# The last piece's tail takes in an output product and a convolution as diagonal products, and the front's loads and conversions are put in another order

## The chip, the cores and the metric

The kernel runs on one core of a Trainium2 chip. The time is the device time of one launch in microseconds, the median of three runs. The engines are named as in the profile: TensorE (PE), VectorE (DVE), ScalarE (ACT), GpSimd (POOL) and SyncE (SP), which issues all the DMAs here.

## The reference

Three layers follow each other for 4 batches of 768 tokens with 384 channels: a gated linear attention with 8 heads of 48, a layer with a Fourier mix and an MLP of 1536 hidden channels, and a gated projection with a short causal convolution.

```python
for t in range(S):
    state = alpha[:, :, t, :, None] * state + np.einsum('bhd,bhe->bhde', k[:, :, t], v[:, :, t])
    y[:, :, t] = np.einsum('bhd,bhde->bhe', q[:, :, t], state)
...
mixed = np.real(np.fft.fft(np.fft.fft(x, axis=1), axis=2))
u = x + mixed
un = (u - mu) / np.sqrt(var + 1e-06)
ch = np.maximum(un @ w_ch1, 0.0) @ w_ch2
x = u + ch
...
for k in range(K):                       # K = 5
    gate_pre += conv_w[k][None, None, :] * xp[:, k:k + S, :]
gate = 1.0 / (1.0 + np.exp(-gate_pre))
out = gate * (x @ w_val) @ w_out
```

## The kernel before

Each batch goes through four stages: attention (six steps of 128 tokens), the Fourier mix, the MLP and the gate. MLP and gate work on pieces of 256 tokens, three to a batch, so there are twelve pieces. Channels lie on the partitions, in three blocks of 128 (`KD`). A product of full precision is made of three products with halves: high weight by high value, low weight by high value, high weight by low value (`mm3`, L648; high and low are `xh`, `xl`).

**The front** is the attention of batch 0 and the start of its Fourier mix, up to the first MLP product. `first` (L384) goes through eight strings of letters, `FIRST` (L44), one string a step, and emits for each letter one part: `A` VectorE's scans of a step, `B` its transposes and score products, `U` and `S` the state products (L335) and the state's update (L346, L351), `D` the output products (L366, L372), `0` to `2` transposes back (`turn`, L472), `f` to `h` the folds, `p` and `r` parts of the Fourier product (`dft_part`, L514). The letters `q`, `v` and `a` issue the loads of queries with keys and decays, of `vu` and of `va`. `l` issues up to four loads of weight chunks (L199), as far as buffers are free. `w` takes the next part of a weight conversion.

Weights come as 64-bit numbers in 24 chunks of 128x384 for w1 and w2, 7 more for the last weights. For a chunk VectorE makes a 32-bit number with three operations (L222, L225, L229), ScalarE rounds it to the high half (L233), and the low half is the rest: in the front two products of TensorE with the identity and with its negative (L242, L243) and a ScalarE copy (L244), later one subtraction on VectorE (L238). In the front `w` converts up to two staged chunks in three parts. From the first MLP piece on `convert_one` converts one chunk at every second step, together with the rest of the chunk before. The tap weights `cw` are a small chunk of 128x15 among the last seven.

**The order of the work.** The program is emitted in one order and each engine works through its instructions in that order; waits come from buffers and data. In the pieces, `run` (L846) emits an MLP step by step, and between the steps the next batch's attention, the norm of the next piece, the gate of the piece before and conversions.

**The end.** The gate of piece 10 ends with the output product, two times nine products of 384 columns (L759), a copy and a transfer; these lie between steps of the MLP of piece 11. Then `last_gate` (L766) does the gate of piece 11 alone. The MLP's last products finish channel block 2 first, then 0 and 1 (`LAST`). For block 2 the five taps of the convolution run on ScalarE and GpSimd (L792, L794), for the others on VectorE (L800, L802); the low halves `xl` come from GpSimd and VectorE; then the value products (L811), the sigmoids, the gating (L816), the halves of the gated values (L817, L819) and the output product (L825). PSUM tiles have the names `aux` (4 buffers), `mm` (2) and `ch`.

Of the kernel before, what the change touches and what calls it, by code (L numbers as in the profile page):

```python
# [43 lines left out]
FIRST = ("Alwwlqwwl", "BlaAlUwqwSvl", "lBDAwwllUaqvlSw", "BwlwwAwDallwUvSq", "AllylDBwUSavx", "BwAlDUSlawwv", "BawDlU0lSww1lfl", "lDg2wpllrh")  # L44
# [20 lines left out]
class Main:  # L65
# [630 lines left out]
    def gate(self, b, p):  # L696
# [45 lines left out]
        for j in range(KD):  # L742
# [6 lines left out]
            yield  # L749
        yield  # L750
# [14 lines left out]

    def last_gate(self, b, p):  # L766
# [8 lines left out]
        xh, xl = (self.pair(b * NPC + p + 2, [P, KD, NK]) for _ in range(2))  # L775
        gh, gl = (self.pair(b * NPC + p + 3, [P, KD, NK]) for _ in range(2))
# [3 lines left out]

        for j in LAST:
# [3 lines left out]
            if j == LAST[1]:  # L785
                nc.gpsimd.tensor_tensor(out=xl[:, j], in0=x2[:, j], in1=xh[:, j].bitcast(F32), op=ALU.subtract)
            if j != LAST[0]:
                continue
            for k in range(KC):
                xs, w = tap(j, k)  # L790
                m = self.t([P, NK], "tmp", 3) if k else gs[:, j]
                nc.scalar.activation(out=m, in_=xs, func=AF.Copy, scale=w)  # L792
                if k:
                    nc.gpsimd.tensor_tensor(out=gs[:, j], in0=gs[:, j], in1=m, op=ALU.add)  # L794
            nc.gpsimd.tensor_tensor(out=xl[:, j], in0=x2[:, j], in1=xh[:, j].bitcast(F32), op=ALU.subtract)
        for k in range(KC):
            for j in LAST[1:]:
                xs, w = tap(j, k)
                if k == 0:
                    nc.vector.tensor_scalar(out=gs[:, j], in0=xs, scalar1=w, scalar2=None, op0=ALU.mult)  # L800
                else:
                    nc.vector.scalar_tensor_tensor(out=gs[:, j], in0=xs, scalar=w, in1=gs[:, j],  # L802
                                                   op0=ALU.mult, op1=ALU.add)
        j = LAST[2]
# [8 lines left out]
        for j in LAST:  # L813
            nc.scalar.activation(out=gs[:, j], in_=gs[:, j], func=AF.Sigmoid)
# [316 lines left out]
```

## Time and profile before

| | |
|---|---|
| median of 3 runs | 639.39 us (634.35 to 640.05) |
| the profiled execution's own time | 641.17 us |
| its span, first to last instruction | 639.1 us |
| granted clock of TensorE, mean | 0.959 |
| busy: TensorE, VectorE, ScalarE, GpSimd | 585.1, 430.1, 244.5, 155.4 us |

The busy times are sums over stages with different limits. The profiled execution lies 1.8 us above the median; a time that is worked out from its rows is set against 641.17 first. A granted clock of 1.00 is 2.4 GHz, one of 0.50 is 1.2 GHz, and a value between them is a mix of both in that stretch.

### The profile page before, as it was taken

What the parts mean: (1) busy time and instruction counts of PE and PEld (TensorE: products, weight loads), DVE (VectorE), ACT (ScalarE), POOL (GpSimd) and SP (SyncE); (2) the same over time, 40 slices, a digit from 0 to 9 for tenths busy, and PEclk for the clock granted to TensorE, in tenths of its full rate; (3) what the DMA queues carried; (4) which work ended last, traced back from release to release, by engine and by line L of the source; (5) the groups of instructions that cost most, each with busy time, mean ns of one, the idle gap of its engine ahead of it and who ended that gap; (6) DMA issues with size and microseconds to landing.
All of it is one profiled execution on the core that took longest, in us unless ns stands there. A gap on an engine that the chain in (4) does not pass through costs nothing.

```text
span 639.1 us, 15952 instructions
## 1 busy us (share of the span) xinstructions
PE 585.1 (92%) x6626; PEld 547.0 (86%) x6626; DVE 430.1 (67%) x951; ACT 244.5 (38%) x582; POOL 155.4 (24%) x332
## 2 busy tenths in 40 slices
PE   3767899797999999999999999999999999999984
PEld 2546768686998899899999999899998999999973
DVE  6988778899836658975763939878556444453642
ACT  2333442224463264353543243434443343423221
POOL 0000215103126033123321324323231232322220
PEclk9868998789899999999999999999999999999996
DMA  9746351646143346533425346533321122000000
GB/s 339 279 137 229 108 173 11 200 144 164 51 138 71 124 125 115 171 99 89 135 75 92 103 125 142 157 110 94 115 63 48 49 71 88 15 9 26 9 27 30
DMA packets 29602, 69.50 MB, mean 109 GB/s; under 512 B 5200, under 2 KB 15952, under 8 KB 29520
## 3 DMA queue, kind: packets, MB, share of 16 engines
q1 hardware_dynamic: 29520, 68.38, 36.5%
q8 instruction: 54, 0.88, 0.6%
q14 instruction: 28, 0.23, 0.1%
HBM read 63.64 MB, written 4.73 MB: 107 GB/s over the span
## 4 chain that ended last, share of the span: by engine, by line
PE 68%; DVE 21%; DMA 4%; POOL 2%; issue 2%; ACT 2%; SPq 1%; DVEq 0%; POOLq 0%
PE ch L651 7%; PE mm L651 7%; PE ch L653 7%; PE ch L652 6%; PE mm L653 6%; PE mm L652 6%; PE aux L759 5%; PE aux L514 3%; PE aux L559 3%; DVE w L295 3%; DVE w L288 2%; PE aux L318 2%; PE aux L651 2%; PE aux L653 2%; PE aux L652 2%
## 5 line engine op out<-in xcount | busy, mean ns | idle before, releaser
L651 PE MATMUL ch<-hh,w2h 128*128 128x256 f32 x432 | 130.2, 301 | 0.2 <-ACT hh L672 0.2
L651 PE MATMUL mm<-hl,w1h 128*128 128x256 f32 x432 | 128.5, 298 | 1.0 <-ACT hl L608 1.0
L653 PE MATMUL ch<-hlo,w2h 128*128 128x256 f32 x432 | 122.9, 285 | 1.5 <-DVE hlo L674 1.5
L652 PE MATMUL ch<-hh,w2l 128*128 128x256 f32 x432 | 122.8, 284 | 0.0
L653 PE MATMUL mm<-hl,w1h 128*128 128x256 f32 x432 | 121.4, 281 | 0.0
L652 PE MATMUL mm<-hl,w1l 128*128 128x256 f32 x432 | 121.3, 281 | 0.0
L674 DVE SCALAR_TENSOR_TENSOR hlo<-mm,hh 128x512 fp32r<-128x512 f32 x72 | 49.5, 687 | 88.4 <-ACT hh L672 88.2
L651 PEld LDWEIGHTS mm<-hl,w1h 128*128 128x128 f32 x432 | 81.8, 189 | 4.0 <-ACT hl L608 1.4
L651 PEld LDWEIGHTS ch<-hh,w2h 128*128 128x128 f32 x432 | 82.5, 191 | 2.8 <-ACT hh L672 0.4
L653 PEld LDWEIGHTS ch<-hlo,w2h 128*128 128x128 f32 x432 | 82.7, 191 | 1.9 <-DVE hlo L674 1.9
L652 PEld LDWEIGHTS ch<-hh,w2l 128*128 128x128 f32 x432 | 82.7, 191 | 0.8
L652 PEld LDWEIGHTS mm<-hl,w1l 128*128 128x128 f32 x432 | 82.0, 190 | 0.8
L653 PEld LDWEIGHTS mm<-hl,w1h 128*128 128x128 f32 x432 | 81.9, 190 | 0.3 <-DVE hl L611 0.3
L672 ACT ACTIVATE hh<-mm 128x512 fp32r<-128x512 f32 x72 | 42.5, 591 | 58.7 <-PE mm L653 58.4
L726 DVE SCALAR_TENSOR_TENSOR ga<-u,cw,ga 128x256 f32<-128x256 f32 x132 | 58.0, 499 | 0.0
L748 POOL TENSOR_TENSOR hl<-ga,hl 128x256 fp32r<-128x256 f32 x33 | 25.5, 779 | 97.2 <-ACT hl L747 97.2
L617 POOL TENSOR_TENSOR tmp<-tmp,tmp 128x256 f32<-128x256 f32 x24 | 20.3, 846 | 101.3 <-ACT tmp L616 100.4
L380 POOL COPY x<-x 128x1 f32<-128x1 f32 x24 | 11.8, 493 | 123.8 <-ACT x L377 123.8
L318 PEld LDWEIGHTS aux<-w 48*64 48x64 f32 x768 | 27.5, 149 | 15.6 <-issue 8.2
L318 PE MATMUL aux<-w 48*64 48x64 f32 x768 | 30.9, 237 | 10.7 <-DVE w L298 6.0
L759 PE MATMUL aux<-wvo,hl 128*128 128x384 f32 x198 | 38.4, 337 | 0.0
L759 PEld LDWEIGHTS aux<-wvo,hl 128*128 128x128 f32 x198 | 33.8, 188 | 0.1
(178 smaller groups left out, 1166.1 us busy)
## 6 DMA issues: line engine op xcount, KB each, us to landing
qka<-in_qka_dram SPq DMA_DIRECT2D x23, 772.5 KB, 5.9
ck<-in_w_dram SPq DMA_DIRECT2D x24, 384.0 KB, 3.4
vu<-in_vu_dram SPq DMA_DIRECT2D x24, 192.0 KB, 3.6
u<-in_w_dram SPq DMA_DIRECT2D x12, 384.0 KB, 6.2
va<-in_va_dram SPq DMA_DIRECT2D x24, 192.0 KB, 4.0
ck<-in_al_dram SPq DMA_DIRECT2D x12, 384.0 KB, 3.3
out_dram<-ga SPq DMA_DIRECT2D x24, 192.0 KB, 1.9
w<-in_cs_dram SPq DMA_DIRECT2D x6, 579.0 KB, 5.3
```

The source lines that it names most:

```text
L295: nc.vector.tensor_tensor_scan(out=pre, data0=al[:, : A_W - 1], data1=self.starts, initial=0.0, op0=ALU.mult, op1=ALU.add)
L318: nc.tensor.matmul(out=sc[j * 64 : j * 64 + 64, cs], lhsT=kt[hs, cs], rhs=qt[hs, cs], start=True, stop=True)
L514: self.nc.tensor.matmul(out=pa[: d1 - d0, g * 193 : g * 193 + n], lhsT=self.eo[g][:, t, m, d0:d1], rhs=self.cs[g][:, t, m, :n], start=t == ...
L617: nc.gpsimd.tensor_tensor(out=ss, in0=ss, in1=sq, op=ALU.add)
L651: nc.tensor.matmul(out=out, lhsT=w[0][:, k, cols], rhs=xh, start=first, stop=False)
L652: nc.tensor.matmul(out=out, lhsT=w[1][:, k, cols], rhs=xh, start=False, stop=False)
L653: nc.tensor.matmul(out=out, lhsT=w[0][:, k, cols], rhs=xl, start=False, stop=last)
L672: nc.scalar.activation(out=hh, in_=hp, func=AF.Relu)
L674: nc.vector.scalar_tensor_tensor(out=hl, in0=hp, scalar=0.0, in1=hh.bitcast(F32), op0=ALU.max, op1=ALU.subtract)
L726: nc.vector.scalar_tensor_tensor(out=gs[:, j], in0=xs, scalar=w, in1=gs[:, j], op0=ALU.mult, op1=ALU.add)
L748: nc.gpsimd.tensor_tensor(out=gl[:, j], in0=gs[:, j], in1=gh[:, j].bitcast(F32), op=ALU.subtract)
L759: nc.tensor.matmul(out=po[:, :DM], lhsT=lh[:, k, ts], rhs=rh[:, k, :], start=n == 0, stop=n == 8)
```

## The change

At the end: the gate of piece 10 stops ahead of its output product and leaves its two operands to the last gate. `last_gate` runs this product itself, one half (`before(0)`) ahead of the value products and one (`before(1)`) behind them. The convolution of block 1 (`LAST[2]`) becomes five products of TensorE in FP32, each tap a diagonal matrix times a shifted slice; GpSimd builds the diagonals in `taps`. The taps of blocks 2 and 0 and all low halves are VectorE's, and the value products go block by block of their input. The last product takes the blocks in the order 1, 2, 0. In the front `FIRST` is another table.

```diff
-FIRST = ("Alwwlqwwl", "BlaAlUwqwSvl", "lBDAwwllUaqvlSw", "BwlwwAwDallwUvSq", "AllylDBwUSavx", "BwAlDUSlawwv", "BawDlU0lSww1lfl", "lDg2wpllrh")
+FIRST = ("Aqwwlwl", "aBwAqUwwSv", "BAwDwUaqvSw", "wBAwwwaDlwUvSq", "AlyllDBwUSavx", "BwAlDUSlawwwv", "aBwDlU0Sw1lf", "lgDwp2hr")
...
+        if self.tail and b * NPC + p + 2 == B * NPC:
+            self.rest = (b, p, gh, gl)
+            return
...
+    def taps(self):
+
+        self.diag = self.t([P, KC, P], "qka", 2)
+        for k in range(KC):
+            self.nc.gpsimd.tensor_scalar(out=self.diag[:, k], in0=self.ident, scalar1=self.cw[:, LAST[2], k : k + 1],
+                                         scalar2=None, op0=ALU.mult)
...
         for j in LAST:
-            nc.vector.tensor_tensor(out=gs[:, j], in0=ch[j], in1=rs, op=ALU.mult)
-            nc.vector.tensor_tensor(out=x2[:, j], in0=x2[:, j], in1=gs[:, j], op=ALU.add)
+            m = self.t([P, NK], "tmp", 3)
+            nc.vector.tensor_tensor(out=m, in0=ch[j], in1=rs, op=ALU.mult)
+            nc.vector.tensor_tensor(out=x2[:, j], in0=x2[:, j], in1=m, op=ALU.add)
             nc.scalar.activation(out=xh[:, j], in_=x2[:, j], func=AF.Copy)
...
+            if j == LAST[0]:
+                conv(j, 0)
+        before(0)
+        values(xh, LAST[0])
         for k in range(KC):
...
+            nc.tensor.matmul(out=cv[:, :NK], lhsT=self.diag[:, k], rhs=tap(LAST[2], k)[0],
+                             start=k == 0, stop=k == KC - 1)
+        for k in LAST[1:]:
+            values(xh, k)
         for j in LAST:
...
+            nc.vector.tensor_tensor(out=xl[:, j], in0=x2[:, j], in1=xh[:, j].bitcast(F32), op=ALU.subtract)
+            conv(LAST[0], 1 + LAST.index(j))
+        for k in LAST:
+            values(xl, k)
+        before(1)
+        conv(LAST[1], 0)
+        conv(LAST[0], 4)
+        for k in range(1, KC):
+            conv(LAST[1], k)
+        os = self.t([P, NK // P, DM], "w", 5)
+        nc.scalar.activation(out=os[:, 0], in_=po[0][:, :DM], func=AF.Copy)
+        nc.scalar.activation(out=gs[:, LAST[2]], in_=cv[:, :NK], func=AF.Sigmoid)
+        nc.scalar.activation(out=gs[:, LAST[0]], in_=gs[:, LAST[0]], func=AF.Sigmoid)
+        nc.scalar.activation(out=gs[:, LAST[1]], in_=gs[:, LAST[1]], func=AF.Sigmoid)
+        order = (LAST[2], LAST[0], LAST[1])
```

Here `before(t)` is the nine products of the old L759 for one half, `values(x, k)` the value products of input block `k` for all three output blocks, and `conv(j, k)` one tap on VectorE.

TensorE at the end of the program, before: the last channel products of the MLP (`ch`), then the value products (`aux`, `mm` from the halves `hl` and the weights `wvo`).

```order
L651 MATMUL ch_1063_7787<-hh_8031,w2h 128x256
L652 MATMUL ch_1063_7787<-hh_8031,w2l 128x256
L653 MATMUL ch_1063_7787<-hlo_8033,w2h 128x256
L811 MATMUL aux_8113<-hl_1087_8072,wvo_1089 128x256 x2
L811 MATMUL mm_8111<-hl_1087_8072,wvo_1089 128x256 x2
L811 MATMUL mm_8112<-hl_1087_8072,wvo_1089 128x256 x2
```

The same place now, from the end of the first half of the old output product (L801) on; `qka` holds the halves of the values and the diagonals.

```order
L801 MATMUL aux_8051<-wvo_1179,hl_1071_7869 128x384 x2
L801 MATMUL aux_8051<-wvo_1179,hl_1072_7870 128x384
L807 MATMUL aux_8055<-qka_8048,wvo_1179 128x256 x2
L807 MATMUL mm_8053<-qka_8048,wvo_1179 128x256 x2
L807 MATMUL mm_8054<-qka_8048,wvo_1179 128x256 x2
L828 MATMUL aux_8056<-u_6193,qka_8041 128x256 x5
L807 MATMUL aux_8055<-qka_8048,wvo_1179 128x256 x2
```

Nine products that stood in the MLP now follow the last channel product, and the five diagonal products stand behind the value products of the first input block.

VectorE in the front, before: step 3, from its scans (L288 to L298) to the state's update (L346); `hl_61_386` takes two chunks, and two more were converted just ahead of the scans.

```order
L288 SCALAR_TENSOR_TENSOR w_377<-qka_199,ends 128x520
L292 RECIPROCAL starts<-w_377 128x8
L293 TENSOR_TENSOR w_378<-qka_199,w_377 128x512
L295 SCALAR_TENSOR_TENSOR w_377<-qka_199,starts 128x520
L298 TENSOR_TENSOR w_378<-qka_199,w_377 128x512
L222 TENSOR_SCALAR hl_61_386<-u_103 128x384 x2
L225 SCALAR_TENSOR_TENSOR hl_61_386<-u_103,hl_61_386 128x384 x2
L229 SCALAR_TENSOR_TENSOR hl_61_386<-u_103,hl_61_386 128x384 x2
L346 TENSOR_TENSOR sp_459<-st_322,pend_278 128x192
```

The same step now; `hl_51_330` is the step's only chunk.

```order
L222 TENSOR_SCALAR hl_51_330<-hl_8_113 128x384
L225 SCALAR_TENSOR_TENSOR hl_51_330<-hl_8_113,hl_51_330 128x384
L319 TENSOR_TENSOR w_333<-aux_340,mask 128x512
L288 SCALAR_TENSOR_TENSOR w_358<-qka_177,ends 128x520
L292 RECIPROCAL starts<-w_358 128x8
L293 TENSOR_TENSOR w_359<-qka_177,w_358 128x512
L295 SCALAR_TENSOR_TENSOR w_358<-qka_177,starts 128x520
L298 TENSOR_TENSOR w_359<-qka_177,w_358 128x512
L229 SCALAR_TENSOR_TENSOR hl_51_330<-hl_8_113,hl_51_330 128x384
L346 TENSOR_TENSOR sp_443<-st_320,pend_245 128x192
```

In this step one chunk is converted in place of four. Up to the first MLP product it is 15 chunks in place of 18, and the three others are converted in the first two pieces.

VectorE in the first MLP piece, before: the second attention step's scans there, with the conversion of `cw` ahead of their last operation (L298).

```order
L295 SCALAR_TENSOR_TENSOR w_1297<-qka_1002,starts 128x520
L222 TENSOR_SCALAR u_103<-u_103 128x15
L225 SCALAR_TENSOR_TENSOR u_103<-u_103 128x15
L229 SCALAR_TENSOR_TENSOR cw<-u_103 128x15
L298 TENSOR_TENSOR w_1298<-qka_1002,w_1297 128x512
L674 SCALAR_TENSOR_TENSOR hlo_1330<-mm_1305,hh_1328 128x512
```

The same place now.

```order
L295 SCALAR_TENSOR_TENSOR w_1276<-qka_974,starts 128x520
L222 TENSOR_SCALAR hl_205_1294<-u_103 128x384
L225 SCALAR_TENSOR_TENSOR hl_205_1294<-u_103,hl_205_1294 128x384
L229 SCALAR_TENSOR_TENSOR hl_205_1294<-u_103,hl_205_1294 128x384
L238 TENSOR_TENSOR w2l<-hl_197_1236,w2h 128x384
L298 TENSOR_TENSOR w_1277<-qka_974,w_1276 128x512
```

A weight chunk stands where `cw` stood, and `cw` is converted behind the next attention step's scans.

## Rows read from the trace of the kernel before

**Rows 1.** Busy time by stretch; start:end, length, each engine, clock, DMA share, GB/s.

```profile
0.00:70.00 70.00, 44.86 (x813) 34.70 (x813) 58.14 (x132) 22.84 (x63) 5.49 (x17) 0.85 0.71 248
...
88.00:170.00 82.00, 68.72 (x924) 63.49 (x924) 75.75 (x151) 26.38 (x64) 19.17 (x39) 0.88 0.46 128
...
580.00:615.00 35.00, 35.00 (x290) 35.00 (x289) 14.49 (x33) 7.89 (x14) 7.53 (x19) 1.00 0.08 16
615.00:639.10 24.10, 12.21 (x60) 10.53 (x59) 11.89 (x24) 5.94 (x15) 4.73 (x6) 0.78 0.06 21
```

**Rows 2.** Timeline of VectorE, 36 to 49 us; start, length, instructions, [idle before, released by].

```profile
36.61 0.62 DVE L222 TENSOR_SCALAR hl<-u 128x384 int32<-128x384 int32 x2
...
39.02 0.35 DVE L346 TENSOR_TENSOR sp<-st,pend 128x192 f32<-128x192 f32 x1
...
48.58 0.36 DVE L351 TENSOR_TENSOR st<-mm,sp 128x192 f32<-128x192 f32 x1 [3.20 <-PE mm L335]
```

**Rows 3.** Timeline of TensorE, 24 to 89 us.

```profile
24.11 1.11 PE L335 MATMUL mm<-vu,w 64*64 64x48 f32 x32 [3.22 <-DMA vu<-in_vu_dram]
...
44.26 1.65 PE L242 MATMUL ch<-hl,ident 128*128 128x384 f32 x2
...
47.75 0.77 PE L335 MATMUL mm<-vu,w 64*64 64x48 f32 x32
...
69.99 0.44 PE L472 MATMUL aux<-ident,x 128*128 128x128 f32 x2 [1.69 <-POOL x L380]
...
88.99 0.38 PE L651 MATMUL mm<-hl,w1h 128*128 128x256 f32 x1 [0.96 <-ACT hl L608]
```

**Rows 4.** Timeline of VectorE, 97 to 119 us.

```profile
97.39 0.35 DVE L222 TENSOR_SCALAR hl<-w 128x384 int32<-128x384 int32 x1
...
99.31 0.15 DVE L625 TENSOR_SCALAR nv<-aux 128x2 f32<-128x2 f32 x1
...
118.41 0.17 DVE L222 TENSOR_SCALAR u<-u 128x15 int32<-128x15 int32 x1 [2.13 <-DMA u<-in_cw_dram]
```

**Rows 5.** Waits of TensorE, 88 to 165 us; who for whom, total, times, longest.

```profile
PE aux L318 <- DVE w L607: 4.6, 1, 4.6
PE aux L318 <- DVE w L298: 3.5, 1, 3.5
```

**Rows 6.** Timeline of the output product of piece 10, 604 to 608 us.

```profile
604.93 1.75 PE L759 MATMUL aux<-wvo,hl 128*128 128x384 f32 x9
...
606.35 0.19 PEld L651 LDWEIGHTS ch<-hh,w2h 128*128 128x128 f32 x1
606.52 0.28 PE L651 MATMUL ch<-hh,w2h 128*128 128x256 f32 x1
...
607.59 1.73 PE L759 MATMUL aux<-wvo,hl 128*128 128x384 f32 x9
```

**Rows 7.** Timeline of the tail, 616 to 633 us.

```profile
616.48 0.28 PE L653 MATMUL ch<-hlo,w2h 128*128 128x256 f32 x1
...
620.19 4.74 DVE L802 SCALAR_TENSOR_TENSOR ga<-u,cw,ga 128x256 f32<-128x256 f32 x8
...
626.00 0.42 DVE L816 TENSOR_TENSOR ga<-aux,ga 128x256 f32<-128x256 f32 x1 [0.74 <-PE aux L811]
...
626.93 5.56 PE L825 MATMUL aux<-wvo,hl 128*128 128x384 f32 x18 [0.61 <-ACT hl L817]
...
632.53 0.56 DVE L832 COPY ga<-aux 128x384 f32<-128x384 f32 x1 [4.44 <-PE aux L825]
```

**Rows 8.** Busy time by stretch in the tail, columns as in rows 1.

```profile
623.00:625.30 2.30, 0.33 (x3) 0.13 (x2) 2.26 (x6) 0.74 (x2) 0.00 (x0) 0.90 0.01 4
625.30:631.00 5.70, 5.08 (x16) 4.74 (x17) 2.09 (x6) 1.16 (x4) 0.00 (x0) 0.50 0.01 3
```

**Rows 9.** Chain of work that ended last, the first norm's FP32 products; start, length, what.

```profile
86.73 1.31 PE aux L593 x6
```

**Rows 10.** Timeline of VectorE, taps of piece 10's convolution.

```profile
596.16 2.46 DVE L726 SCALAR_TENSOR_TENSOR ga<-u,cw,ga 128x256 f32<-128x256 f32 x6
```

More of the change, by code (lines that the diff above doesn't have):

```diff
@@ L43 @@
 LAG_RS = 3
[L44 removed]
+FIRST = ("Aqwwlwl", "aBwAqUwwSv", "BAwDwUaqvSw", "wBAwwwaDlwUvSq", "AlyllDBwUSavx", "BwAlDUlSawwwv", "aBwDlU0Sw1lf", "lgDwp2hr")
 ORDER = "Bb.Aa..Dt.m.Cvc.q."
@@ L774, in last_gate @@
         gs = self.t([P, KD, NK], "ga", 1)
-        xh, xl = (self.pair(b * NPC + p + 2, [P, KD, NK]) for _ in range(2))
-        gh, gl = (self.pair(b * NPC + p + 3, [P, KD, NK]) for _ in range(2))
+        xhl = self.t([P, 2, KD, NK], "qka", 2, F32R)
+        xh, xl = xhl[:, 0], xhl[:, 1]
+        gh, gl = (self.pair(b * NPC + p + 1, [P, KD, NK]) for _ in range(2))
         def tap(j, k):
             return u[:, j, o + k : o + k + NK], self.cw[:, j, k : k + 1]
+        b1, p1, gh1, gl1 = self.rest
@@ new lines, in last_gate, with before, values @@
+        po = [self.aux() for _ in range(NK // P)]
+        va = [self.mm(), self.mm(), self.aux()]
+        cv = self.aux()
+        def before(t):
+            for k in range(KD):
+                for n, (lh, rh) in enumerate(((gh1, self.wo[0]), (gh1, self.wo[1]), (gl1, self.wo[0]))):
+                    nc.tensor.matmul(out=po[t][:, :DM], lhsT=lh[:, k, t * P : (t + 1) * P], rhs=rh[:, k, :],
+                                     start=k == 0 and n == 0, stop=k == KD - 1 and n == 2)
+        def values(x, k):
+            for j in LAST:
+                for w in self.wv if x is xh else self.wv[:1]:
+                    nc.tensor.matmul(out=va[j][:, :NK], lhsT=w[:, k, j * P : (j + 1) * P], rhs=x[:, k],
+                                     start=x is xh and k == LAST[0] and w is self.wv[0], stop=x is xl and k == LAST[2])
@@ L784, in last_gate @@
             nc.scalar.activation(out=xh[:, j], in_=x2[:, j], func=AF.Copy)
[L785 to L794, printed above, removed]
@@ L795, in last_gate @@
-            nc.gpsimd.tensor_tensor(out=xl[:, j], in0=x2[:, j], in1=xh[:, j].bitcast(F32), op=ALU.subtract)
-        for k in range(KC):
[L797 to L803, printed above, removed]
@@ L804, in last_gate @@
-        j = LAST[2]
-        nc.vector.tensor_tensor(out=xl[:, j], in0=x2[:, j], in1=xh[:, j].bitcast(F32), op=ALU.subtract)
-        va = [self.mm(), self.mm(), self.aux()]
-        for x, ws in ((xh, self.wv), (xl, self.wv[:1])):
-            for k in LAST:
-                for j in LAST:
-                    for w in ws:
-                        nc.tensor.matmul(out=va[j][:, :NK], lhsT=w[:, k, j * P : (j + 1) * P], rhs=x[:, k],
-                                         start=x is xh and k == LAST[0] and w is ws[0], stop=x is xl and k == LAST[2])
@@ L816, in last_gate @@
+        order = (LAST[2], LAST[0], LAST[1])
+        for j in order:
             nc.vector.tensor_tensor(out=gs[:, j], in0=va[j][:, :NK], in1=gs[:, j], op=ALU.mult)
             nc.scalar.activation(out=gh[:, j], in_=gs[:, j], func=AF.Copy)
-        for j in LAST:
+        nc.scalar.activation(out=os[:, 1], in_=po[1][:, :DM], func=AF.Copy)
+        for t in range(NK // P):
+            r = b1 * S + p1 * NK + t * P
+            nc.sync.dma_start(out=self.ap["out"][r : r + P, :], in_=os[:, t])
+        for j in order:
@@ L819, in last_gate @@
             nc.vector.tensor_tensor(out=gl[:, j], in0=gs[:, j], in1=gh[:, j].bitcast(F32), op=ALU.subtract)
         po = [self.aux() for _ in range(NK // P)]
-        for k in LAST:
+        for k in order:
             for t in range(NK // P):
@@ L825, in last_gate @@
                     nc.tensor.matmul(out=po[t][:, :DM], lhsT=lh[:, k, ts], rhs=rh[:, k, :],
-                                     start=k == LAST[0] and n == 0, stop=k == LAST[2] and n == 2)
+                                     start=k == order[0] and n == 0, stop=k == order[2] and n == 2)
         for t in range(NK // P):
@@ L854, in run @@
         self.check_jobs()
+        self.tail = True
         self.head, self.pa, self.n_rest = True, None, 0
@@ L920, in run @@
                 pass
+        self.taps()
         self.last_gate(*pieces[-1])
@@ L1017, in general @@
         nc = self.nc
+        self.tail = False
         with ExitStack() as c:
```

9 lines of the change are left out of this document (7 added, 2 removed).

## The prediction

> **What bounds the kernel now.** I read first the busy time by stretch [rows 1]. From 0 to 70 us (attention of the first batch, called the front here) VectorE works 58.1 of 70 us and TensorE only 44.9. From 88 to 170 us (the first two pieces of the MLP, with weight conversions and the attention of the next batch beside them) VectorE works 75.8 of 82 us and TensorE loses 13 us. From 580 to 615 us TensorE is without a gap at full clock. From 615 us to the end it works 12.2 of 24.1 us at a mean granted clock of 0.78. So there are three limits: VectorE in the front, VectorE again from 88 to 170 us, and a chain through all engines in the tail. The timelines and the waits then tell who waits for whom in each.
>
> **Tail.** The change removes 18 products of the piece before the last (L759) from the last MLP, two runs of nine. From the start of the first run to the next MLP product it is 1.59 us (604.93 to 606.52) [rows 6], for both 3.18. TensorE has no gap there [rows 1], so the last channel product, which ends at 616.76 us (616.48 + 0.28) [rows 7], ends at 613.58. The products that feed it are not nearer: each takes hidden values that were made a step earlier, as before.
>
> Before, TensorE then waited at each step for ScalarE, GpSimd and VectorE: it was busy 0.33 of 2.3 us from 623.0, and from 625.3 to 631 the granted clock was 0.50, the lower level of 1.2 GHz [rows 8]. The 18 output products L825 ran there, 5.56 us from 626.93 [rows 7].
>
> After, work that depends on nothing late stands in these holes. I add it up in TensorE's new order, at the prices of rows at full clock: nine products of 384 columns 1.59, nine of 256 columns 1.07 (606.52 to 607.59) [rows 6], six FP32 passes of 256 columns 1.31 [rows 9], which make three products, so 0.44 each.
> - first half of the old output product: 1.59
> - six value products of the first block: 0.71
> - five diagonal FP32 products: 2.18
> - twelve value products: 1.43, and nine with the low parts: 1.07
> - second half of the old output product: 1.59
> - 18 output products at full clock: 3.18
>
> That is 11.75 us, and TensorE ends at 625.33, where the last copy began at 632.53 [rows 7]: 7.2 us earlier. Copy, output transfer and end follow as before.
>
> VectorE must keep up. After 613.58 it has 16 operations of 128x256: four products or sums, three subtractions, a first tap and eight further taps. A tap takes 0.41 in the middle of the kernel (six in 2.46) [rows 10] and 0.59 in the old tail, where GpSimd worked beside it (eight in 4.74) [rows 7]; the new tail has no GpSimd work, so I take 0.41 for all 16. That gives 6.6 us, to 620.2; with 0.59 for the eight it would be 621.6. The value products end at 613.58 + 6.98 = 620.56. From the first gating product to the first output product it took 0.93 us before (626.00 to 626.93) [rows 7], so that one is ready at 621.5 (622.5 with slow taps), and TensorE wants it at 622.15. The low part of it comes after three gating products, about 0.1 to 0.3 us late. The second accumulator of the output product needs the copy of the old second half, which ScalarE does about 0.6 us after that half ends; it costs 0.1. I take **7.0 us** for the tail, 4.5 to 8 with the slow taps and a partial loss of clock. The five scalings that build the diagonals stand on GpSimd ahead of the last gate; it is busy 7.5 of the 35 us before 615 [rows 1], and they are wanted at about 616.
>
> The diagonals are FP32. The row for FP32 passes [rows 9] is 0.22 us a pass, weight loads included. The Trainium skill ("TensorE: Matmul & The Clock Gate", section on weight-path performance modes) says that the fast weight load is off for FP32 data, which speaks against this block. If its ten loads stood bare at the 0.19 us of a load in [rows 6], the block would cost 1.9 us more and the tail would gain 5.1. In [rows 9] six such loads lie covered, and that row decides.
>
> **Front.** Three weight chunks fewer are converted before the MLP: 15 of 24 in place of 18. A chunk is 1.2 us on VectorE (two from 36.61 to 39.02) [rows 2], so 3.6 us leave the engine that bounds the front. One of the two residual pairs (L242, L243) in front of the state product L335 goes: two stood there from 44.26 to 47.75 [rows 3] and VectorE waited 3.20 us for what followed [rows 2]; half of it, 1.7 us, goes. Third, a part of the Fourier product now stands ahead of the last transposes, which waited 1.69 us for GpSimd [rows 3]; it fills that hole, 1.7 us. From there to the MLP's first product at 88.99 TensorE has the same work. Together **7.0 us**, at least 3.5 (the 3.6 alone), at most 9 if the other short waits of the front go too. Of the moved loads, two `va` loads are issued ahead of the products that free their buffer, so SyncE stands there until these are done; behind it wait only weights and the loads of the next step. The weights come later on its queue, and the `vu` load of step 3 comes behind four of them (rival 1).
>
> **MLP, first two pieces.** The three chunks come back here as single conversions of four VectorE operations, 1.92 us each (97.39 to 99.31) [rows 4]: 5.8 us on an engine that is busy 92% of the time [rows 1], and TensorE's longest waits there, 4.6 and 3.5 us, are for it [rows 5]. In return the tap weights (cw) are converted later: VectorE waited 2.13 us for their load [rows 4], and now a chunk that has long landed stands in this place, while cw is converted one attention step later. So 5.8 - 2.1 = **3.7 us** are given back; the bounds are 1 (the other idle time of VectorE, some 4 us of the 82, takes part of it) and 7 (nothing of the wait goes, and TensorE comes back at the lower clock from longer waits). Nothing hides it: the last of the three stands ahead of the attention step for which TensorE waited those 3.5 us, so the delay reaches it. After 170 us TensorE is again the limit, and the difference is carried to the end.
>
> **Sum.** 7.0 - 3.7 + 7.0 = 10.3 us. The profiled execution took 641.17 us (span 639.1), which becomes 630.9. The median of the runs shown, 639.39, is 1.8 below it, so the forecast is **629.0 us**.
>
> **Rivals.**
> 1. *The front's data come late.* The `vu` load of step 3 now lies behind four weight loads of 0.39 MB (128 rows of 768 words of 4 bytes). At 248 GB/s, the front's mean [rows 1], these take 6.3 us. Once before, TensorE waited 3.22 us for such a load (24.11) [rows 3]. If it does so again, the front gains 3.5, about what the MLP gives back, and only the tail is left: 632.6. The Trainium skill ("DMA: Bandwidth & Descriptors", section on queues, rings and completion order) says that an engine takes a ring's descriptors in order, so that load would indeed wait for all four. Against it: the product that needs it is reached some 9 us after the loads' issue, since VectorE's scans come first.
> 2. *VectorE's waits absorb the conversions.* The MLP gives back 1 us and the front gains 9: 624.4.
> 3. *The tail does not hold the clock.* If a hole opens ahead of the last 27 products and they run at 1.2 GHz, 4.8 us of the 7.0 are lost: 633.8. That happens if the taps take 0.59 us and the gating starts late.
> 4. *Slower.* The fourth quarter of w1 (three chunks) is now done two steps ahead of its first use, not eight. If TensorE waits at each of the three as long as it waited there at worst, 4.6 us [rows 5], and comes back once at the lower clock, as from 625.3 to 631 (5.7 us at half speed, so 2.9 lost) [rows 8], the MLP gives back 5.8 + 13.8 + 2.9 = 22.5 us, more than the 14.0 that front and tail save: 647.9. It decides from 14 us. Against it: TensorE already trails VectorE there by its attention steps.
> 5. *The change does not do what it says:* the moved output product only changes its place, since TensorE is full either way. That holds if the holes of the tail stay; it then leaves the MLP with 3.2 us and comes back with 3.2, and the time is near that of rival 3.
>
> **How the numbers follow.** Forecast 0.52, rival 1 0.20, rival 2 0.12, rivals 3 and 5 0.11, rival 4 0.05. The range runs from 623 (rival 2, with 1 us for the scatter of runs, 634.35 to 640.05) to 636.5 (both low bounds of front and tail together: 3.5 - 5 + 4.5 = 3.0). About 1%, or 6.4 us, is what a measurement of this kernel can tell from no change; that is below 633.0. The forecast and rival 2 lie under it, rival 1 does so about every second time: faster 0.77, within 0.18, slower 0.05.
>
> **What would show it.** Right: the first MLP product near 82 us; no VectorE wait for cw; the last channel product some 6 to 7 us earlier than 616; from there TensorE without a hole over 0.3 us and at a granted clock of 1.0 to its end; about 11.7 us from the last channel product to the last output product. Wrong: a first MLP product later than 85 us, waits of TensorE for L238 in the first piece, or a granted clock of 0.5 in the tail.

## The result and the profile after

The changed kernel takes **631.63 us** (median of 13 runs, 628.89 to 636.51), the kernel before 639.39 (634.35 to 644.0) beside it: a ratio of 0.9894, with a 95% interval of 0.9866 to 0.9923. The forecast was 629.0 us, with a range of 623.0 to 636.5. The ratios here are taken from the fast executions alone and are not the quotients of the medians shown. So the sign and the range were right. Of the expected 10.4 us, 7.8 came by the medians and 6.8 (4.9 to 8.6) by the ratio, so a quarter to a third did not come. The profiled execution of the changed kernel took 634.48 us (span 632.7), 2.9 above its median.

I read it in the order of the prediction: the stretches first, then the timelines. The windows of the changed kernel answer to [rows 1]; the second stretch is, as there, about that from the first MLP product to the first gate:

```profile
0.00:70.00 70.00, 48.83 (x846) 39.74 (x847) 58.15 (x135) 21.61 (x61) 6.51 (x19) 0.88 0.68 244
81.70:170.20 88.50, 70.19 (x920) 64.78 (x921) 81.48 (x163) 27.26 (x66) 19.30 (x39) 0.84 0.44 124
580.00:615.00 35.00, 35.00 (x298) 35.00 (x298) 16.18 (x39) 8.18 (x17) 11.21 (x25) 1.00 0.06 8
615.00:632.70 17.70, 11.95 (x76) 11.36 (x74) 9.30 (x24) 4.67 (x12) 0.00 (x0) 0.92 0.14 50
```

The last row is the tail: 17.7 us in place of 24.1, and the mean granted clock is 0.92. The second row is the surprise. The stretch of 82 us before is now 88.5 us long; VectorE was busy 75.8 us in it and is busy 81.5 us now, still 92%. So nearly all of the added time (5.7 of 6.5 us) is added VectorE work.

**Front.** TensorE's timeline of the changed kernel, for [rows 3]:

```profile
62.23 1.54 PE L514 MATMUL mm<-wvo,w 128*97 128x193 f32 x8
64.92 0.82 PE L472 MATMUL aux<-ident,x 128*128 128x128 f32 x6
...
81.69 0.39 PE L651 MATMUL mm<-hl,w1h 128*128 128x256 f32 x1 [0.96 <-ACT hl L608]
```

A Fourier product (L514) now stands ahead of the last transposes (L472), and these no longer wait for GpSimd. The first MLP product is at 81.69, before at 88.99: 7.3 us earlier.

**MLP, first two pieces.** Three waits here were not in the trace before. The first group shows TensorE, the second VectorE:

```profile
106.78 0.39 PE L652 MATMUL mm<-hl,w1l 128*128 128x256 f32 x1 [2.61 <-DVE w1l L238]
...
159.76 0.28 PE L653 MATMUL mm<-hl,w1h 128*128 128x256 f32 x1
166.98 0.58 PE L651 MATMUL aux<-hl,wvo 128*128 128x256 f32 x1 [6.93 <-ACT x L377]
167.35 0.42 PE L652 MATMUL aux<-hl,wvo 128*128 128x256 f32 x1
```

```profile
124.77 0.17 DVE L222 TENSOR_SCALAR u<-u 128x15 int32<-128x15 int32 x1
...
128.48 0.69 DVE L319 TENSOR_TENSOR w<-aux,mask 128x512 f32<-128x512 f32 x1 [1.54 <-PE aux L318]
```

At 106.78 TensorE waits for a weight's low part. At 124.77 the tap weights (cw) are converted without the wait of 2.13 us of [rows 4], but at 128.48 VectorE waits 1.54 us for TensorE, which is late. At 166.98 TensorE has stood 6.93 us in front of the first value product, and the row is 0.58 long. The windows show the clock after these waits:

```profile
102.70:122.70 20.00, 15.18 (x165) 13.37 (x164) 18.97 (x36) 6.97 (x19) 1.97 (x3) 0.71 0.57 134
...
160.00:167.00 7.00, 0.07 (x2) 0.02 (x1) 6.90 (x14) 1.03 (x5) 0.01 (x1) 0.67 0.08 25
167.00:172.40 5.40, 5.40 (x25) 5.40 (x26) 2.94 (x8) 4.86 (x9) 1.18 (x3) 0.50 0.10 10
```

In the 7 us of the wait VectorE works 6.9 us. Then TensorE runs 5.4 us at a granted clock of 0.50, which is 1.2 GHz. In the trace before, the first value product stood behind other work without a wait:

```profile
168.05 0.28 PE L651 MATMUL aux<-hl,wvo 128*128 128x256 f32 x1
```

Who holds the value product is seen on ScalarE's timeline:

```profile
161.61 0.22 ACT L291 ACTIVATE pend<-w 128x8 f32<-128x8 f32 x1 [3.10 <-DVE w L288]
166.18 0.52 ACT L233 ACTIVATE wvo<-u 128x384 fp32r<-128x384 f32 x1 [4.36 <-DVE u L229]
166.61 0.31 ACT L377 ACTIVATE x<-aux 128x192 f32<-128x192 f32 x1
```

The copy L377 frees the accumulator that the value product needs. It stands in ScalarE's queue behind the rounding L233 of a late weight, and that waits for VectorE's conversion.

**Where the gain went** is best followed by a mark that stands in every execution: the rounding of the hidden values (L672 on ScalarE, 72 times). The first came at 92.94 before and comes at 85.64 after (-7.3), the tenth at 171.78 and 171.31 (-0.5), the eleventh at 180.41 and 182.08 (+1.7). Then the difference stands still: 600.32 and 602.01 at the seventieth. So the MLP's first pieces took back not 3.7 but 9.0 us. The first and the eleventh mark, before and after:

```profile
92.94 0.58 ACT L672 ACTIVATE hh<-mm 128x512 fp32r<-128x512 f32 x1
180.41 0.60 ACT L672 ACTIVATE hh<-mm 128x512 fp32r<-128x512 f32 x1 [0.60 <-PE mm L653]
...
85.64 0.58 ACT L672 ACTIVATE hh<-mm 128x512 fp32r<-128x512 f32 x1
182.08 0.60 ACT L672 ACTIVATE hh<-mm 128x512 fp32r<-128x512 f32 x1 [0.60 <-PE mm L653]
```

The windows divide these 9.0 us, first the kernel before, then the changed one. Each first row goes from the first MLP product to the first value product, each second one from there to the eleventh mark:

```profile
88.99:168.05 79.06, 66.74 (x906) 61.54 (x906) 72.98 (x145) 24.25 (x61) 19.17 (x39) 0.87 0.45 126
168.05:180.41 12.36, 12.36 (x192) 11.74 (x191) 6.15 (x16) 7.06 (x16) 3.77 (x6) 1.00 0.25 66
...
81.69:166.98 85.29, 66.98 (x906) 61.57 (x906) 79.44 (x158) 24.08 (x62) 19.02 (x38) 0.85 0.46 129
166.98:182.08 15.10, 15.10 (x190) 14.48 (x191) 5.69 (x14) 8.66 (x18) 4.08 (x7) 0.81 0.15 41
```

Up to the first value product it takes 6.2 us longer. VectorE works 6.5 us more there, and TensorE no more than before. Behind it TensorE has no gap in either trace and nearly the same products, but its mean granted clock is 0.81 in place of 1.00, and it takes 2.7 us longer.

**Tail.** TensorE's and VectorE's timelines of the changed kernel, for [rows 7]:

```profile
615.04 0.28 PE L653 MATMUL ch<-hlo,w2h 128*128 128x256 f32 x1
615.16 1.72 PE L801 MATMUL aux<-wvo,hl 128*128 128x384 f32 x9
...
617.43 2.32 PE L828 MATMUL aux<-u,qka 128*128 128x256 f32 x10
...
622.08 1.73 PE L801 MATMUL aux<-wvo,hl 128*128 128x384 f32 x9
623.65 3.31 PE L862 MATMUL aux<-wvo,hl 128*128 128x384 f32 x18
```

```profile
619.40 2.44 DVE L815 SCALAR_TENSOR_TENSOR ga<-u,cw,ga 128x256 f32<-128x256 f32 x5
622.35 0.42 DVE L849 TENSOR_TENSOR ga<-mm,ga 128x256 f32<-128x256 f32 x1 [0.50 <-ACT ga L846]
```

TensorE has no hole: 11.64 us from the end of the last channel product (615.32) to the end of the last output product (626.96), where 11.75 was forecast, and the granted clock there is 1.00:

```profile
615.32:626.96 11.64, 11.63 (x73) 11.04 (x72) 8.42 (x23) 4.35 (x12) 0.00 (x0) 1.00 0.10 36
```

Ahead of it, between the seventieth mark and the last one, the 18 moved products are missing: the last mark is at 612.53 before and at 611.15 after, so +1.7 has become -1.4, which is 3.1 us. From the last channel product to the end it is 17.4 us, before 22.3. The tail is worth 3.1 + 4.9 = 8.0 us.

The sum of the two profiled executions: -7.3 + 9.0 - 8.0 = -6.3 us, and the spans differ by 6.4.

### The profile page after: what moved, and what is told of

Same layout as the page of the kernel before. It is cut to its first block, busy times and chain, and to the rows that moved or that the text cites. A ratio compares the mean times of both kernels' runs of the same rounds, so it can differ in the third digit from the quotient of the medians.

```text
span 632.7 us, 15932 instructions
## 1 busy us (share of the span) xinstructions
PE 583.0 (92%) x6627; PEld 547.2 (86%) x6627; DVE 430.4 (68%) x956; ACT 240.8 (38%) x574; POOL 155.7 (25%) x331
## 4 chain that ended last, share of the span: by engine, by line
PE 73%; DVE 19%; DMA 3%; issue 2%; ACT 2%; POOL 1%; SPq 0%; DVEq 0%; POOLq 0%
PE ch L651 7%; PE mm L651 7%; PE ch L653 7%; PE ch L652 7%; PE mm L653 6%; PE mm L652 6%; PE aux L762 5%; PE aux L514 4%; PE aux L559 3%; PE aux L318 3%; DVE w L295 2%; DVE ga L726 2%; DVE w L288 2%; PE aux L651 2%; PE aux L366 2%; PE aux L652 2%
## 5 line engine op out<-in xcount | busy, mean ns | idle before, releaser
L651 PEld LDWEIGHTS mm<-hl,w1h 128*128 128x128 f32 x432 | 82.7, 191 | 4.1 <-ACT hl L608 1.4
L653 PEld LDWEIGHTS mm<-hl,w1h 128*128 128x128 f32 x432 | 82.8, 192 | 0.3 <-DVE hl L611 0.3
L672 ACT ACTIVATE hh<-mm 128x512 fp32r<-128x512 f32 x72 | 42.4, 589 | 55.4 <-PE mm L653 55.2
L380 POOL COPY x<-x 128x1 f32<-128x1 f32 x24 | 13.1, 546 | 124.9 <-ACT x L377 124.9
L651 PE MATMUL aux<-hl,wvo 128*128 128x256 f32 x99 | 28.8, 290 | 6.9 <-ACT x L377 6.9
L762 PE MATMUL aux<-wvo,hl 128*128 128x384 f32 x180 | 34.9, 337 | 0.0
```

The costliest lines, as they stand in the source:

```text
L651: nc.tensor.matmul(out=out, lhsT=w[0][:, k, cols], rhs=xh, start=first, stop=False)
L653: nc.tensor.matmul(out=out, lhsT=w[0][:, k, cols], rhs=xl, start=False, stop=last)
L672: nc.scalar.activation(out=hh, in_=hp, func=AF.Relu)
L762: nc.tensor.matmul(out=po[:, :DM], lhsT=lh[:, k, ts], rhs=rh[:, k, :], start=n == 0, stop=n == 8)
```

## Experiments

My theory after reading the traces (A): VectorE bounds the stretch up to the first gate, and each conversion moved there costs its time on VectorE; the clock adds some. The main rival (B): ScalarE's queue order makes the wait of 6.93 us, and VectorE's work is not what counts. Each ratio is to the kernel before on the same chip, with its 95% interval. The runs e5 to e8 are from another chip than e1 to e4 and e9 to e12; across chips only the ratios are compared. "Marks" are the first and the eleventh L672 of the one profiled execution.

**Each part alone.** Only the order of the front, with the old tail:

```diff
-FIRST = ("Alwwlqwwl", "BlaAlUwqwSvl", "lBDAwwllUaqvlSw", ...
+FIRST = ("Aqwwlwl", "aBwAqUwwSv", "BAwDwUaqvSw", ...
```

> The kernel before with the new order of the front's loads and conversions, and the old tail. Theory A (VectorE gives the front's gain back: three conversions of 1.92 us, 5.8 us, come back in a stretch in which VectorE has no gap, and a second stretch of TensorE at granted clock 0.5 costs about 2 more): as long as before, 638 to 641.5 us. The prediction on record (3.3 us net): 636.1 us. Rival B (ScalarE's queue order alone makes TensorE wait 6.9 us at the first value product): also about 639 here; B is told from A by e4_round_pool.

Measured: 640.04 us against 638.31, a ratio of 1.0035 (1.0005 to 1.0065). Marks 85.78 and 182.12, as in the changed kernel. The front's new order by itself gains nothing; it loses 2 us (0.3 to 4.1), as theory A expected.

The new tail with the old order of the front is the opposite edit.

> The new tail with the old order of the front. If the two parts add and the tail is worth what the two profiles show (3.1 us of moved products and 5.0 us from the last hidden values to the end): 631.3 us. The prediction on record (7.0 us): 632.4 us. If the front's new order was worth 3 us in the whole change, this one takes about 634.5 us.

Measured: 630.16 against 638.31, 0.9877 (0.9844 to 0.9910), 7.9 us. In its trace TensorE goes from the last channel product (609.61) to the last output product (621.25) in 11.64 us, as in the changed kernel. So all that the change gains comes from the tail.

**Is VectorE the bound, or ScalarE's order?** First the low parts on GpSimd:

```diff
-                    nc.vector.tensor_tensor(out=l, in0=r, in1=h.bitcast(F32), op=ALU.subtract)
+                    nc.gpsimd.tensor_tensor(out=l, in0=r, in1=h.bitcast(F32), op=ALU.subtract)
```

> The changed kernel, with the subtraction that makes the low part of a weight (L238) on GpSimd wherever VectorE did it, 17 times 0.55 us, 9.4 us less on VectorE from 82 to 170 us. Theory A (VectorE bounds this stretch): 4 to 8 us faster than the changed kernel, 623.5 to 627.5 us. If VectorE does not bound it: within 1 us of 631.6. Against a gain: GpSimd needs about 1.1 us for each (0.73 us for 256 columns in the profile after), some 19 us more beside its 19.3 us there, and a product that waits for a low part would wait longer.

Measured: 636.73 against 638.31, 0.9959 (0.9933 to 0.9984): slower than the changed kernel. The expected gain is missed, and the groups by line show why. First this kernel on GpSimd and VectorE, then a row of VectorE's timeline in it, then the groups of the changed kernel on VectorE (mean ns of one behind the busy time):

```profile
L238 POOL TENSOR_TENSOR w2l<-hl,w2h 128x384 fp32r<-128x384 f32 x6 | 7.4, 1241 | 4.3 <-ACT w2h L233 4.3
L238 POOL TENSOR_TENSOR wvo<-u,wvo 128x384 fp32r<-128x384 f32 x6 | 6.2, 1037 | 8.4 <-ACT wvo L233 8.4
L346 DVE TENSOR_TENSOR sp<-st,pend 128x192 f32<-128x192 f32 x9 | 4.8, 536 | 0.2
```

```profile
96.92 1.16 DVE L222 TENSOR_SCALAR hl<-w 128x384 int32<-128x384 int32 x1 [2.19 <-POOL w2l L238]
```

```profile
L238 DVE TENSOR_TENSOR w2l<-hl,w2h 128x384 fp32r<-128x384 f32 x6 | 3.3, 548 | 0.0
L346 DVE TENSOR_TENSOR sp<-st,pend 128x192 f32<-128x192 f32 x9 | 3.2, 356 | 0.2
```

A subtraction takes about twice as long on GpSimd, and VectorE waits for it once (2.19 us at 96.92). Some of VectorE's own operations grow beside it: of the nine L346 the three that ran beside a GpSimd subtraction took 0.79 to 1.09 us, the other six 0.35 to 0.36 as before. So VectorE is busy 78.4 us from the first MLP product to the first value product, hardly less than the 79.4 of the changed kernel. Work that goes to GpSimd does not leave VectorE free here. So this run does not tell whether VectorE is the bound.

Then only the rounding of the six late weights, so that ScalarE's queue is not held:

```diff
+                if ts is None:
+                    nc.gpsimd.tensor_copy(out=h, in_=r)
+                else:
+                    nc.scalar.activation(out=h, in_=r, func=AF.Copy)
-                nc.scalar.activation(out=h, in_=r, func=AF.Copy)
```

> The changed kernel, with the rounding of the six late conversions (wv and wo, L233, 0.52 us each) on GpSimd in place of ScalarE, so that on ScalarE nothing that waits for VectorE's conversions stands ahead of the copies L377 which free the accumulators of the first value products. VectorE's work is the same. Rival B (the queue order of ScalarE is the cause): the wait of 6.9 us goes and the time falls by 5 to 7 us, to 624.6 to 626.6. Theory A (VectorE is the bound): the wait closes, but only the second stretch at half clock comes back, 0 to 2.5 us: 629 to 631.6.

Measured: 630.21 against 638.31, 0.9863 (0.9827 to 0.9900). In TensorE's timeline of this kernel the wait has closed and another has opened, for VectorE:

```profile
159.40 0.35 PE L654 MATMUL aux<-hl,wvo 128*128 128x256 f32 x1 [1.60 <-ACT x L380]
165.53 1.11 PE L313 MATMUL aux<-ident,w 128*128 128x128 f32 x4 [2.71 <-DVE st L354]
```

Marks (here of L675, the same rounding) 84.73 and 177.53, 92.8 us apart, where the changed kernel has 96.4. The value product no longer waits 6.93 but 1.60 us, and yet the time falls by 1 to 2 us at most (0.9863 against the 0.9894 above and the 0.9876 of the changed kernel's second run below, with intervals that overlap), not by 5 to 7. VectorE's work is the same, and TensorE now waits for it elsewhere. Rival B is out as the main cause.

**Conversions out of the stretch.** The wo weights are needed only by the first output product. Here they wait until the first gate's value products are issued:

```diff
-                if self.weights_left(False) and n % (SOON if self.weights_left(True) else DEFER) == 0:
+                if self.n_done < (N_WV if self.hold else N_JOBS) and n % (SOON if self.weights_left(True) else DEFER) == 0:
...
-        while self.weights_left(False):
+        while self.n_done < N_WV:
             self.weight_step()
...
+        self.hold = False
...
+        while self.weights_left(False):
+            self.weight_step()
+            for _ in range(4):
+                self.weight_load(True)
         os = gs.rearrange("p a b -> p (a b)").rearrange("p (a b) -> p a b", b=DM)
```

(N_WV is 28, and `hold` begins as true.)

> The changed kernel, with the last three conversions (wo, which only the first output product needs) held back until the first gate's value products are done, so that two of them (2 x 1.92 us and a subtraction of 0.55, 4.4 us of VectorE) leave the stretch up to 171 us and nothing is taken out of the work. Theory A (VectorE bounds the stretch up to the first gate, and TensorE after it): 4.4 us come back, and some of the half clock: 625 to 628 us, 0.978 to 0.983 of the kernel before. Rival E (the delay only moves to where the conversions then stand): no change, 0.989.

Measured: 627.52 against 638.96, 0.9827 (0.9784 to 0.9870); the changed kernel on the same chip (below) 630.47 and 0.9876. Marks 86.09 and 173.65, 87.6 us apart, about what it was before the change (87.5). In TensorE's timeline the value product now stands without a wait and at full clock, and part of the delay comes back at the output product:

```profile
160.32 0.28 PE L651 MATMUL aux<-hl,wvo 128*128 128x256 f32 x1
...
176.95 1.97 PE L767 MATMUL aux<-wvo,hl 128*128 128x384 f32 x5 [2.63 <-DVE wvo L238]
```

By the thirteenth mark (195.91, before 198.45) 4.2 of the 6.8 us that it lay ahead of the kernel before at the eleventh are lost again: this wait, and behind it a granted clock of 0.84 from 178 to 184 us. So both theory A and a part of rival E hold: nothing but the place of three conversions was changed, and the median is 3 us lower. The two intervals still overlap, and the spans of the two profiled executions are only 0.7 us apart (628.4 and 629.1), this one being among the slowest of its six.

**Three chunks back in the front.**

```diff
-FIRST = ("Aqwwlwl", "aBwAqUwwSv", "BAwDwUaqvSw", "wBAwwwaDlwUvSq", ...
+FIRST = ("Aqwwlwl", "aBwAqUwwSvl", "BAwDwUaqvlSw", "wBAwwlwaDlwUvSq", ...
```

> The changed kernel with three calls of the weight loads put back into the front's order, so that 18 chunks are converted before the MLP, as in the kernel before, and the rest of the new order stays. Theory A (a chunk costs 1.2 us in the front and 1.92 us in the stretch that VectorE bounds, and the longer waits there bring half clock): first MLP product 3.6 us later than in the changed kernel, 5.8 us less VectorE work from 82 to 170 us, 2 to 4 us faster in all: 0.983 to 0.986 of the kernel before. Rival C (the gain of the front came from the loads that were left out of it, not from the three chunks): the front falls back to the old one, and the time is that of the new tail alone, 0.988.

Measured: 629.11 against 638.07, 0.9872 (0.9843 to 0.9901). Marks 89.78 and 175.70: the front is 4.1 us later than in the changed kernel's first profile, the stretch takes 85.9 in place of 96.4 us. The first value product has no wait here (163.22), and the granted clock behind it is 1.00: both losses came with the three conversions. On ScalarE no rounding L233 stands just ahead of L377 here, so this run does not tell theory A from rival B. In the times it is not told from the changed kernel (0.9894 and 0.9876), nor from rival C: inconclusive. There is no sign that leaving the three chunks out of the front saves anything.

The same three letters, together with the edit of e9_wo_later:

> As e9_wo_later, with the three chunks put back into the front as in e5_three_chunks_back. Theory A: the two gains are of the same kind (VectorE's work up to 171 us) and add as long as VectorE bounds the stretch: 0.975 to 0.981 of the kernel before. If the stretch is no longer bound by VectorE once wo is later, the chunks in the front only cost there: as e9_wo_later or up to 3 us slower.

Measured: 627.01 against 638.96, 0.9819 (0.9781 to 0.9857): not told from e9_wo_later. All six of its times (625.44 to 628.92) lie below all six of the changed kernel on this chip (629.28 to 632.25, below). Marks 91.27 and 172.19, only 80.9 us apart.

And together with the edit of e4_round_pool:

> e5_three_chunks_back with the rounding of the six late conversions on GpSimd, as in e4_round_pool. Theory A: VectorE's work is that of e5, the order on ScalarE costs at most a stretch at half clock: 0 to 2 us faster than e5_three_chunks_back, 0.984 to 0.988 of the kernel before. Rival B (ScalarE's order is the cause of what was given back): 4 us or more faster than e5_three_chunks_back, 0.981 or less.

Measured: 629.94 against 638.96, 0.9877 (0.9840 to 0.9915): no gain over e5_three_chunks_back. This says little about rival B, since in e5_three_chunks_back the wait of the first value product is gone already.

**The changed kernel again**, without an edit, on the chip of the last three:

> The changed kernel itself, once more beside e9 to e11 on one chip. All theories: 0.987 to 0.992 of the kernel before, and its profile shows whether the first MLP product (81.69 us) and the first hidden values of the third piece (182.08 us) of the first profile stand again or move by 1 to 3 us.

Measured: 630.47 against 638.96, 0.9876 (0.9837 to 0.9915). Its marks are 83.25 and 178.48, not 85.64 and 182.08.

These marks move between executions of one order. With the front's new order (but for one letter in e6) and the stretch behind it unchanged there are six profiles (the changed kernel twice, e1, e6, e7, e8), with the old order two (the kernel before, e2):

| | first L672 | eleventh L672 | between |
|---|---|---|---|
| new order, 6 profiles | 83.25 to 85.78, mean 84.9 | 178.48 to 182.12, mean 180.2 | 93.9 to 96.4, mean 95.3 |
| old order, 2 profiles | 90.43 and 92.94, mean 91.7 | 176.32 and 180.41, mean 178.4 | 85.9 and 87.5, mean 86.7 |

So the front is worth 6.8 us and the stretch takes back 8.6. The net of 1.8 against the change is what the front alone measured (2 us slower).

The runs that move conversions show what sets the length of the stretch (us, from the windows of each trace):

| | first MLP product to first value product | VectorE busy in it | from there to the eleventh L672 | granted clock there |
|---|---|---|---|---|
| before | 79.1 | 73.0 | 12.4 | 1.00 |
| changed kernel | 85.3 | 79.4 | 15.1 | 0.81 |
| changed kernel again | 84.2 | 79.4 | 15.0 | 0.82 |
| e5_three_chunks_back | 77.4 | 73.0 | 12.5 | 1.00 |
| e9_wo_later | 78.2 | 72.9 | 13.3 | 1.00 |
| e10_wo_later_chunks_back | 71.3 | 67.1 | 13.6 | 1.00 |
| e4_round_pool | 78.6 | 75.0 | 18.1 | 0.81 |

Up to the first value product the length follows VectorE's work, with 3.6 to 6.1 us more in each. In e4_round_pool the product comes earlier, but the conversions that are left and half the clock then stand behind it, and the sum is 96.7, against 100.4 and 99.2 in the changed kernel's two profiles and 91.4 before.

**The transposes.** The Fourier product behind them again:

```diff
-..., "lgDwp2hr")
+..., "lgDw2phr")
```

> The changed kernel with the part of the Fourier product behind the last transposes again, as in the kernel before. By the prediction on record (1.7 us, the wait of the transposes for GpSimd): that wait is back, the first MLP product comes 1.7 us later, 633.3 us (0.992 of the kernel before). If other work fills the place anyway: no change, 0.989.

Measured: 632.47 against 638.07, 0.9924 (0.9899 to 0.9948), which is 0.3% above the changed kernel's with intervals that overlap. The wait is back in its trace, 1.2 us:

```profile
61.38 0.44 PE L472 MATMUL aux<-ident,x 128*128 128x128 f32 x2 [1.22 <-POOL x L380]
...
80.38 0.39 PE L651 MATMUL mm<-hl,w1h 128*128 128x256 f32 x1 [0.96 <-ACT hl L608]
```

But the first MLP product is no later than in the others (79.31 to 81.69 in the two profiles of the changed kernel), so in the profile the term cannot be told from the scatter of the front.

**The tail's two parts.** The convolution block on VectorE in place of the diagonal products (the five products and the scalings are left out, and `conv(LAST[2], k)` stands ahead of the taps of the last block):

```diff
-        for k in range(KC):
-            nc.tensor.matmul(out=cv[:, :NK], lhsT=self.diag[:, k], rhs=tap(LAST[2], k)[0],
-                             start=k == 0, stop=k == KC - 1)
...
+        for k in range(KC):
+            conv(LAST[2], k)
```

> The changed kernel with the last convolution block on VectorE (five operations, one of 0.35 and four of 0.48 us, 2.3 us) in place of the five diagonal FP32 products (2.32 us on TensorE). Theory A (VectorE's taps decide when the gating starts): the gating starts 2.0 to 2.4 us later, TensorE stands some 3 to 4 us ahead of the last output products: 2 us slower with the clock kept, up to 5.5 us if the 18 products run at granted clock 0.5: 633.5 to 637 us (0.992 to 0.998 of the kernel before). Rival D (FP32 products are dear on TensorE, and it bounds the tail): no change or up to 2 us faster.

Measured: 635.49 against 638.07, 0.9959 (0.9936 to 0.9981), some 4 us slower than the changed kernel by the ratios; in the profile the tail from the last L672 is 1.8 us longer (23.3 against 21.5), and where the rest was lost stays open. TensorE waits for the gating, as theory A said, and keeps its clock (timeline, then windows):

```profile
618.83 1.75 PE L800 MATMUL aux<-wvo,hl 128*128 128x384 f32 x9
623.96 3.59 PE L860 MATMUL aux<-wvo,hl 128*128 128x384 f32 x18 [3.38 <-ACT hl L848]
```

```profile
620.40:624.00 3.60, 0.23 (x3) 0.04 (x1) 3.49 (x10) 1.67 (x5) 0.00 (x0) 1.00 0.00 0
624.00:627.60 3.60, 3.55 (x18) 2.98 (x18) 1.13 (x5) 1.44 (x4) 0.00 (x0) 1.00 0.17 59
```

And the output product of the piece before the last in its old place (`self.tail = False`, and both calls of `before` with their copies and transfers left out of the last gate):

> The changed kernel with the output product of the last piece but one back in its old place between the MLP's products, 18 products of 3.18 us. Theory A: the last channel product 3.18 us later, and from there the end only 0.5 us nearer, since VectorE's gating is ready 0.45 us before TensorE wants it: 2.7 us slower, and up to 6 if the hole that opens ahead of the last 18 products brings granted clock 0.5: 634.3 to 637.6 us (0.993 to 0.998 of the kernel before). Rival 5 on record (the product only changes place): no change, 0.989.

Measured: 634.86 against 638.07, 0.9951 (0.9930 to 0.9972), 3.6 us slower than the changed kernel by the ratios. From the last L672 to the end it takes 21.4 us, with the moved product 21.5. TensorE then has two holes of 0.8 and 1.0 us in the tail and keeps its clock:

```profile
616.77 2.40 PE L818 MATMUL aux<-u,qka 128*128 128x256 f32 x10 [0.82 <-DVE u L812]
622.69 3.64 PE L845 MATMUL aux<-wvo,hl 128*128 128x384 f32 x18 [1.03 <-ACT hl L837]
```

So the product costs the tail nothing and the MLP 3.1 us: rival 5 is out. Since both of these runs keep the clock in the tail, neither part alone is what keeps it.

## Why the prediction was right, and where it was off

The time lay in the range, but the account behind it was right in two terms of three, and that the time came out so near is in part luck. Front and MLP together were to save 3.3 us; they cost some 2 (e1_front_alone).

**Front, 7.0 us: right**, 7.3 in the first profile and 6.8 over all of them. Two of its three terms were tested. With the three chunks back (e5_three_chunks_back) the first mark is 4.1 us later than in the first profile and 4.9 later than the mean, where 3.6 was the term. The wait at the transposes that comes back is 1.2 us, not 1.7, and its worth in the time stays open.

**MLP, 3.7 us given back: the failed step.** It measured 9.0 us in the first profile and 8.6 in the mean, above the bound of 7. The first half of the term, 5.8, was nearly right: up to the first value product VectorE works 6.5 us more (79.4 against 73.0), of which the three conversions of 1.92 us are 5.8. Two things were wrong. The first is the 2.1 us taken off. The cw wait went as forecast, but other waits took its place, among them one of 1.54 us for TensorE, which was late. VectorE's idle time up to the first value product is 5.9 us, and it was 6.1 before. The second is the clock. TensorE's longest wait moved to the first value product, where I had not looked: 6.93 us, and behind it 5.4 us at half clock. This is the 2.7 us from the first value product to the eleventh mark. So 6.5 - 0.2 + 2.7 = 9.0 stands where I had 5.8 - 2.1.

In [rows 1] and [rows 5] VectorE's share of 92% was already the sign that what is added to this stretch is paid in full, and in the trace before the first value product followed TensorE's other work at 168.05 without a wait, so a longer queue ahead of it had nothing to hide behind. What I gave as the upper bound (nothing of the wait goes, and the clock falls) was the case that came, and priced too low. The low end of the range did not even use that bound: it was added up with 5, not with 7.

That the three conversions are the cause shows in e5_three_chunks_back, where both parts are back at 77.4 and 12.5 us. That the 6.93 us as such are not the loss shows in e4_round_pool. Work taken out of the stretch and put behind the first gate (e9_wo_later) shortens it again, but it is not free there either: 4.2 us are lost behind it.

**Tail, 7.0 us: right**, 8.0 in the profile and 7.9 in the times of e2_tail_alone. The sum on TensorE held (11.64 us against 11.75), the moved product gave 3.1 us (3.18 forecast), the clock was kept at 1.00, and the gating was ready in time: ScalarE's first rounded block (L850, 0.42 us from 622.80) ended at about 623.2, and TensorE came to the output product at 623.65. A tap took 0.49 us (five in 2.44), between the two rows I had. Most of the 1 us that came on top is the drain: from the last output product to the end 6.6 us before (632.49 to 639.1) and 5.7 after (626.96 to 632.7), which I had put down as unchanged. The ten FP32 passes of the diagonals took 2.32 us, 1.97 from their start to the next product, so the row on FP32 passes [rows 9] was the better guide. Their ten weight loads lie beside the passes:

```profile
617.32 2.03 PEld L828 LDWEIGHTS aux<-u,qka 128*128 128x128 f32 x10
```

The Trainium skill ("TensorE: Matmul & The Clock Gate", section on weight-path performance modes) says that the fast weight load is off for FP32 data. The 1.9 us that I had estimated for bare loads did not come here.

**The rivals.** Rival 1 (late `vu`) did not come: in the first profile TensorE waited for it once, 3.2 us, as long as it had at 24.11 before [rows 3]. Rival 2 is out: the MLP gave back 9, not 1. Rival 3 did not come; in e7_conv_vector a hole of 3.4 us ahead of the last 18 products did not bring it either. Rival 4 came in its mechanism and not in its size: TensorE waited once, 2.61 us, for a quarter of w1, not three times 4.6. A wait for L238 in the first piece was one of the signs I had named for being wrong. Another sign failed too: the last channel product was to come 6 to 7 us earlier, and it came 1.4 earlier (615.04 against 616.48).

So the time was right because the tail outdid its term by 1 us and the range had room for the 5 us by which the MLP missed its term. Had the tail come in at its own low bound of 4.5, the time would have been 635.1, near the end of the range.

## What to carry to other kernels

Work deferred from one stretch that an engine bounds into another that the same engine bounds is not saved; look for the stretch in which that engine has time to spare (here behind the first value product, where VectorE worked 6.2 of 12.4 us before), and count how late its last consumer is. When an in-order engine gets more to do, follow its queue to the first operation behind it that frees a buffer for TensorE, and add the slow clock after that wait as a term of its own. In a tail, filling TensorE's waits with work that depends on nothing late pays twice: the work disappears from where TensorE was full, and the clock is kept (here 1.00 in the tail, where 5.7 us had run at 0.50).

## What the runs showed of the hardware

- The front of one and the same program ended 2.4 us apart in two executions (first MLP product at 81.69 and 79.31). From 50 to 60 us TensorE was as busy in both (7.74 and 7.75 us), but the granted clock was 0.66 in one and 1.00 in the other. So a difference of 2 us in the front of two single traces need not come from an edit.
- A hole of 3.38 us in TensorE's work in the tail of e7_conv_vector left the granted clock at 1.00 for the 18 products behind it, while the one of 6.93 us after a stretch of other waits was followed by 5.4 us at 0.50.
- A subtraction of 128x384 took 1.04 to 1.24 us on GpSimd (e3_low_part_pool) where VectorE takes 0.55. VectorE's L346 (128x192) took 0.79 to 1.09 us the three times that it ran beside one, and otherwise 0.36.
